# Which engine adds up weights and rows, when slots are read, and the order of row writes, in attention with a mixture of experts

## The chip, the cores and the metric

One core of one Trainium2 chip runs the whole program. The metric is the device time of one execution in microseconds (us), as the median of several runs. The engines are TensorE (PE; its weight loads are PEld), VectorE (DVE), ScalarE (ACT), GpSimd (POOL) and SyncE (SP, which here issues transfers).

## The reference

```python
def _attn_ref(q, k, v, sampled_blocks) -> np.ndarray:
    ...
    scores = scale * np.matmul(q, k.transpose(0, 1, 3, 2))
    ...
    scores = np.where(mask, scores, -1000000000.0)
    ...
    return np.matmul(attn, v).astype(np.float32)
def _moe_ref(x, w_gate, w_noise, noise, w1, w2) -> np.ndarray:
    ...
    logits = x @ w_gate
    noise_scale = np.log1p(np.exp(x @ w_noise))
    noisy_logits = logits + noise_scale * noise
    top2 = np.argpartition(-noisy_logits, 2, axis=1)[:, :2]
    ...
    for e in range(E):
        for k in range(2):
            mask = top2[:, k] == e
            ...
            h = np.maximum(x[mask] @ w1[e], 0.0)
            out[mask] += top2_w[mask, k, None] * (h @ w2[e])
```

The attention has 4 batches of 8 heads, 768 positions of 64, in blocks of 32; its mask leaves each block the blocks beside it, the first, the last and three sampled ones. The rows of its output, with all heads side by side, are the x of the experts: 3072 rows of 512. There are 8 experts (512 to 1024 to 512), and the two weights of a row are a softmax over its two largest gates.

## The kernel before

The first part, up to some 350 us, is the attention; beside it the router picks two experts for each row and scatters, for each expert, row numbers and weights into a table in DRAM (`slots`). The second part runs the experts as **units**: u0 and u1 are two shares of expert 0, u2 is expert 1, and u3 to u8 are experts 2 to 7. A unit has up to 816 rows: six chunks of 128 and one of 48. All products are done in f16 with each f32 operand split into a high and a low half, so that one product is three matmuls.

For a unit, the program reads its slots (`meta`, tile `mt`), makes row numbers of them (`indices`, tile `gi`, on VectorE), gathers the rows of x (`gather`, tile `xg`, an indirect transfer on GpSimd's queue) and transposes them by transfers on SyncE's queue (`xpose`, tiles `xta` and `xtb`). `gather_prev` fetches the rows of the output that earlier units have written (`pv`, GpSimd's queue). **Layer 1** makes h in the tiles `hh` and `hl`. **Layer 2** (`mm2`) makes each chunk of output rows in the PSUM bank `pc`; `finish` weighs it and adds `pv` on VectorE (tile `y`, three buffers), and writes the rows by an indirect transfer on GpSimd's queue (`out_dram<-y,mt`). The narrow chunk of 48 rows is done second, turned after the third, so that two writes come together there.

u0 to u2 do layer 1 straightforwardly (`mm1`, in the order `FORDER`). u3 to u8 are **fast units** (`layer1_fast`): layer 1 is done in 2 x 2 blocks with seven products in place of eight (28 products of 6 matmuls, in the order of the list `PRODUCTS`; the first digit is the group, the second the product). This takes sums and differences of weight blocks (`weight_sums`, tile `ws`, four additions of 256 columns for each of four pieces) and of x (`row_sums`, four of 816 columns; `row_differences`, eight of 408 columns; tile `xf`, one buffer, filled once for each half s of the rows' columns). `row_high` and `row_low` split `xf` into the tile `tb`, on ScalarE and VectorE. Products 4 to 7 read `tb`; the fourth product in the list is the first of these. Inside a group, ScalarE copies partial results into tiles `ta` and `tc`, two buffers each, VectorE adds to them, and `high` and `low` make `hh` and `hl` of them.

Weight pieces (eight of 512 KB an expert) are loaded into `wraw`, three buffers; the high half is made on ScalarE (`high_piece`), the low half on VectorE (`low_piece`), and then the load three pieces on is issued on SyncE (`next_load`).

Every engine works through its own instructions in the order in which the program was written; an engine that waits holds up all that stands behind on it. What is done beside the matmuls is written out in tables: `FRONT` and `FRONT_ROWS` at eight places (hooks) in layer 1, `BACK0` (u2) and `BACK` (u3 on) after each chunk of layer 2. In them h and l are the high and low half of a weight piece, s its sums, g a gather and x a transpose for a unit ahead, rs, rd, rh, rl the row sums, differences, high and low half for the next unit. u2 thus prepares u3 in `BACK0`, where both halves of its rows stand in layer 2; later units do half 0 in layer 1 and half 1 in layer 2. The slots of a unit are read two units ahead, at the third hook of layer 1, and `indices` follows at the fourth. The tiles of `meta` have three buffers, and a buffer is free when the writes of its unit have landed.

## Time and profile before

| | us |
|---|---|
| median of 3 runs | 972.69 (970.95 to 973.55) |
| the profiled run | 964.51 |
| span of the profiled run, first to last instruction | 962.7 |
| PE busy in the span | 830.0 (86%) |
| DVE, ACT, POOL busy | 541.2, 367.0, 467.4 |

Mean granted TensorE clock of the span: 0.94 of full speed. Layer 1 of u2 begins at 443.01 us, its layer 2 at 483.79, u3 at 518.30, and the last matmul ends at 946.8.

How to read the rows below. A row of the timeline has start and duration in us, engine, line, operation, what it writes and reads, a count, and in brackets how long the engine stood idle before and what ended that. SPq, POOLq and the like are an engine's own instruction queue. A row of waits has the waiting engine, tile and line, what it waited for, the total us, the number of times and the longest. A row of a stretch has its bounds, its length, the busy us (and instructions) of PE, PEld, DVE, ACT and POOL, the granted clock as a share of full speed, the DMA share and GB/s. A row of a source line has the operation with its count, and the shortest, median and longest duration in ns. L790 is line 790 of the kernel before.

### The profile page before, as it was taken

The numbers are of one execution on the slowest core, as the hardware profiler recorded it, in microseconds if no ns is written. First come the engines' busy times: TensorE is split into PE (matmuls) and PEld (weight loads), VectorE is DVE, ScalarE is ACT, GpSimd is POOL, SyncE is SP. The second block draws the span as 40 slices with busy tenths as digits, with TensorE's granted clock in tenths as the row PEclk, the third lists the DMA queues.
The fourth block names the chain that finished last, engine by engine and source line by source line (L and its number), as shares of the span: only waits on it lengthen the run. The fifth ranks groups of instructions, "written<-read, shape, count | busy, mean of one in ns | idle before, by whom it ended". The sixth has DMA issues, their size and how long they took to land. (4 is left out here: it accounts for less than half of the span.)

```text
span 962.7 us, 25081 instructions
## 1 busy us (share of the span) xinstructions
PE 830.0 (86%) x9999; PEld 508.6 (53%) x9999; DVE 541.2 (56%) x1088; ACT 367.0 (38%) x672; POOL 467.4 (49%) x758
## 2 busy tenths in 40 slices
PE   5988988888987879985998699898898898999993
PEld 3776766676665756462553354454453453554551
DVE  5666755774564547131457475676675574776620
ACT  5657545544534424020323342532532441533500
POOL 3553465357338312533447636567556556645320
PEclk9999999988878889997999899999998998999997
DMA  7776779677318879448757727837737637832311
GB/s 210 189 203 175 208 194 179 158 190 164 92 41 148 243 170 334 114 154 173 197 127 154 185 85 151 215 114 160 201 105 151 170 109 149 212 103 98 93 36 36
DMA packets 121649, 149.01 MB, mean 155 GB/s; under 512 B 72370, under 2 KB 79283, under 8 KB 121522
## 3 DMA queue, kind: packets, MB, share of 16 engines
q1 hardware_dynamic: 107810, 109.50, 47.4%
q0 software_dynamic: 13712, 37.81, 13.8%
q8 instruction: 81, 1.33, 0.6%
q14 instruction: 46, 0.38, 0.1%
HBM read 107.14 MB, written 26.32 MB: 139 GB/s over the span
## 5 line engine op out<-in xcount | busy, mean ns | idle before, releaser
L1025 PE MATMUL pc<-w,hh 128*128 128x512 f16 x768 | 232.6, 385 | 13.6 <-DVE y L1057 11.5
L1058 POOL DMA_INDIRECT out_dram<-y,mt x56 | 76.4, 1365 | 206.6 <-DVE y L1057 86.7
L978 PEld LDWEIGHTS <-w 128*128 128x128 f16 x1008 | 99.9, 99 | 106.1 <-issue 31.2
L1025 PE MATMUL pc<-w,hl 128*128 128x512 f16 x384 | 147.6, 384 | 0.5 <-DVE hl L950 0.4
L1025 PEld LDWEIGHTS <-hh 128*128 128x128 f16 x768 | 75.3, 99 | 103.5 <-issue 19.5
L273 ACT ACTIVATE p<-ps,m 128x256 f32<-128x256 f32 x192 | 75.3, 475 | 75.4 <-DVE m L270 68.0
L270 DVE TENSOR_REDUCE m<-ps 128x2 f32<-128x512 f32 x96 | 61.8, 685 | 49.6 <-PE ps L224 40.4
L818 DVE SCALAR_TENSOR_TENSOR w<-wraw,w 128x1024 f16<-128x1024 f32 (+1 forms) x62 | 70.2, 1132 | 20.3 <-ACT w L814 20.3
L224 PE MATMUL ps<-kk,q 64*32 64x192 f32 (+1 forms) x1920 | 76.7, 338 | 4.2 <-issue 4.2
L881 POOL DMA_INDIRECT xg<-x_rows,gi x56 | 70.1, 1252 | 20.4 <-issue 12.1
L319 PE MATMUL po<-vb,ptr 128*32 128x68 f32 x1536 | 64.2, 231 | 17.9 <-issue 17.5
L185 POOL COPY kk<-kk 128x128 f32 x264 | 65.0, 296 | 28.9 <-PE ps L224 22.5
L715 POOL DMA_INDIRECT slots<-r_pay,r_sl x48 | 48.0, 1001 | 57.0 <-DVE r_ot L707 48.1
L899 POOL DMA_INDIRECT pv<-out_dram,gi x49 | 52.5, 1071 | 38.5 <-issue 23.5
L319 PE MATMUL po<-va,ptr 128*32 128x68 f32 x1536 | 60.1, 233 | 9.4 <-issue 7.6
L224 PEld LDWEIGHTS ps<-kk,q 64*32 64x32 f32 (+1 forms) x1920 | 51.5, 129 | 30.0 <-issue 24.5
L978 PE MATMUL pa<-tb,w 128*128 128x408 f16 x288 | 57.5, 337 | 9.7 <-ACT tc L966 4.3
L814 ACT ACTIVATE w<-ws 128x1024 f16<-128x1024 f32 x24 | 25.2, 1051 | 106.0 <-POOL ws L790 106.0
L1057 DVE SCALAR_TENSOR_TENSOR y<-pc,mt,pv 128x512 f32<-128x512 f32 x42 | 31.3, 746 | 58.3 <-PE pc L1025 56.0
L1025 PEld LDWEIGHTS <-hl 128*128 128x128 f16 x384 | 38.0, 99 | 48.5 <-issue 3.3
L297 PE MATMUL ps<-r_ident,p 128*128 128x128 f32 x384 | 61.6, 312 | 0.0
L947 ACT ACTIVATE hh<-pa 128x408 f16<-128x408 f32 (+2 forms) x48 | 22.3, 467 | 99.7 <-PE pa L939 94.8
(196 smaller groups left out, 1556.4 us busy)
## 6 DMA issues: line engine op xcount, KB each, us to landing
wraw<-in_moe_w_dram SPq DMA_DIRECT2D x64, 512.0 KB
va<-in_vw_dram SPq DMA_DIRECT2D x16, 768.0 KB
vb<-in_vx_dram SPq DMA_DIRECT2D x176, 64.0 KB
q<-in_qt_dram SPq DMA_DIRECT2D x24, 256.0 KB
out_dram<-zero SPq DMA_DIRECT2D x8, 768.0 KB
va<-in_vx_dram SPq DMA_DIRECT2D x88, 64.0 KB
va<-in_vw_dram SPq DMA_DIRECT2D x8, 576.0 KB
kk<-in_kt_dram SPq DMA_DIRECT2D x9, 512.0 KB
```

Of the source, the lines that this page charges most:

```text
L185: nc.gpsimd.tensor_copy(kk[:, self.row(t, j) + n], flat[:, bass.ds(v[j, n] * P, P)])
L224: mm = lambda o, l, r: nc.tensor.matmul(o, l, r, start=True, stop=True, skip_group_check=True)
L270: nc.vector.tensor_reduce(m[:, par], s[par].rearrange("p (e c) -> p e c", e=2), axis=AX.X, op=ALU.max, negate=True)
L273: nc.scalar.activation(p[:, 2 * e + par], s[par][:, 256 * e:256 * e + 256], AF.Exp, bias=m[:, par, e:e + 1])
L297: nc.tensor.transpose(t[:, e, c], p[:, 2 * e + par, P * c:P * c + P], self.ident)
L319: nc.tensor.matmul(o[32 * j:32 * j + 32, h], d[:, h % 2, h // 2, x, 32 * j:32 * j + 32], self.values(v[:, self.slot(t, j)], 4 * f + h), st ...
L818: self.nc.vector.scalar_tensor_tensor(lo, t, WS, hi, op0=ALU.mult, op1=ALU.subtract)
L881: nc.gpsimd.indirect_dma_start(out=self.xg[0:m, c], out_offset=None, in_=self.x_dram[0:nr], in_offset=bass.IndirectOffsetOnAxis(ap=r["gi"] ...
L899: nc.gpsimd.indirect_dma_start(out=self.pv[0:m, c, :], out_offset=None, in_=self.out, in_offset=bass.IndirectOffsetOnAxis(ap=r["gi"][0:m, ...
L978: nc.tensor.matmul(o, w[:, wt, slot, s * P:s * P + P], mv(s, a), start=i == 0 and p in tail, stop=i == 5, skip_group_check=True)
L1025: nc.tensor.matmul(py, h[:, f, o], w(f)[:, x], start=i == 0, stop=i == last)
L1058: nc.gpsimd.indirect_dma_start(out=self.out, out_offset=bass.IndirectOffsetOnAxis(ap=r["mt"][0:m, c, 0:1], axis=0), in_=y[0:m], in_offset= ...
```

## The change

`weight_sums` moves from GpSimd to VectorE; `row_sums` and `row_differences` move from VectorE to GpSimd. The tile pool of the slots has nine buffers in place of three, and the slots of u4 to u8 are all read in u2's layer 1, with their `indices` there and after u2's first chunk. The writes of rows of one unit are declared independent of one another. The orders `FORDER` and `PRODUCTS` and the tables change; the half-1 row sums of a fast unit stand two steps earlier in layer 2. A load follows its `low_piece` one step later, at the start of the next entry (list `freed`).

```diff
-FORDER = (0, 4, 1, 5, 6, 2, 7, 3)
-PRODUCTS = [(int(a), int(b)) for a, b in ("01 11 02 06 07 17 16 05 14 21 12 04 26 03 15 25 22 31 27 13 36 37 24 35 "
-                                           "32 23 34 33").split()]
+FORDER = (0, 4, 1, 5, 6, 7, 2, 3)
+PRODUCTS = [(int(a), int(b)) for a, b in ("01 11 02 06 12 21 07 16 05 17 04 15 03 14 22 27 26 31 13 24 36 25 37 35 "
+                                           "32 34 23 33").split()]
...
-        self.mp = pool("mmeta", 3)
+        self.mp = pool("mmeta", 9)
...
-        tt = lambda x, y, z, op: nc.gpsimd.tensor_tensor(x, y, z, op=op)
+        tt = lambda x, y, z, op: nc.vector.tensor_tensor(x, y, z, op=op)
...
-        self.nc.vector.tensor_tensor(self.st["xf", u, s][:, j].rearrange("p k c -> p (k c)"), v(0), v(1), op=ALU.add)
+        self.nc.gpsimd.tensor_tensor(self.st["xf", u, s][:, j].rearrange("p k c -> p (k c)"), v(0), v(1), op=ALU.add)
...
-        tt = lambda o, a, b: self.nc.vector.tensor_tensor(o, a, b, op=ALU.subtract)
+        tt = lambda o, a, b: self.nc.gpsimd.tensor_tensor(o, a, b, op=ALU.subtract)
...
-        nc.gpsimd.indirect_dma_start(
+        d = nc.gpsimd.indirect_dma_start(
...
+        for p in r.setdefault("done", []):
+            self.tc.declare_no_dep(d.ins, p.ins, reason="a unit has every row once")
+        r["done"].append(d)
...
-    FRONT_ROWS = ((("x", -6),), (("x", -7),), (), (("rs", 0, 0),), (), (("rs", 0, 1),), (("rd", 0, 0),), (("rd", 0, 1),))
-    BACK0 = ((("h", 0), ("l", 0), ("s", 1)),
-             (("h", 1), ("g", 0)),
-             (("l", 1), ("s", 2), ("rs", 0, 0), ("rs", 0, 1), ("g", 1), ("g", 2)),
-             (("h", 2), ("rd", 0, 0), ("rd", 0, 1), ("rh", 0), ("l", 2), ("s", 3), ("g", 3), ("x", 0)),
-             (("rl", 0), ("rs", 1, 0), ("rs", 1, 1), ("g", 4), ("x", 1), ("x", 2)),
-             (("h", 3), ("rd", 1, 0), ("rd", 1, 1), ("rh", 1), ("l", 3), ("g", 5), ("x", 3)),
+    FRONT_ROWS = ((("x", -6),), (("x", -7),), (), (), (("rs", 0, 0),), (("rs", 0, 1),), (("rd", 0, 0),), (("rd", 0, 1),))
+    BACK0 = ((("h", 0), ("l", 0), ("s", 1), ("h", 1)),
+             (("l", 1), ("g", 0)),
+             (("s", 2), ("h", 2), ("rs", 0, 0), ("rs", 0, 1), ("g", 1), ("g", 2)),
+             (("rd", 0, 0), ("rd", 0, 1), ("rh", 0), ("l", 2), ("s", 3), ("h", 3), ("g", 3), ("x", 0)),
+             (("l", 3), ("rl", 0), ("rs", 1, 0), ("rs", 1, 1), ("g", 4), ("x", 1), ("x", 2)),
+             (("rd", 1, 0), ("rd", 1, 1), ("rh", 1), ("g", 5), ("x", 3)),
              (("rl", 1), ("g", 6), ("x", 4)))
-    BACK = ((("h", 0), ("rh", 0), ("l", 0), ("s", 1), ("g", 0), ("g", 1)),
-            (("h", 1), ("rl", 0), ("g", 2)),
-            (("l", 1), ("s", 2), ("g", 3), ("x", 0)),
-            (("h", 2), ("rs", 1, 0), ("rs", 1, 1), ("l", 2), ("s", 3), ("g", 4), ("x", 1), ("x", 2)),
-            (("rd", 1, 0), ("rd", 1, 1), ("rh", 1), ("g", 5), ("x", 3)),
-            (("h", 3), ("l", 3), ("rl", 1), ("g", 6), ("x", 4)),
+    BACK = ((("h", 0), ("rh", 0), ("l", 0), ("s", 1), ("h", 1), ("g", 0), ("g", 1)),
+            (("rl", 0), ("l", 1), ("rs", 1, 0), ("rs", 1, 1), ("g", 2)),
+            (("s", 2), ("h", 2), ("rd", 1, 0), ("g", 3), ("x", 0)),
+            (("l", 2), ("s", 3), ("h", 3), ("rd", 1, 1), ("g", 4), ("x", 1), ("x", 2)),
+            (("l", 3), ("rh", 1), ("g", 5), ("x", 3)),
+            (("rl", 1), ("g", 6), ("x", 4)),
             ())
...
+    freed = []
...
-        next_load(e, i)
+        freed.append((e, i))
...
-            if u + 2 < nu:
-                if f == 2:
-                    ex.meta(u + 2)
-                if f == 3:
-                    ex.indices(u + 2)
+                if f + 2 > FAST and f + 2 < nu:
+                    ex.meta(f + 2)
+                if f > FAST and f < nu:
+                    ex.indices(f)
...
+        while freed:
+            next_load(*freed.pop(0))
...
+                for v in range(ex.FB, nu):
+                    ex.indices(v)
```

How the change moves instructions, at three places. In the rows below a bracket names the counters that an instruction waits for: DVE, ACT, PE and Pool count the instructions of an engine, DMAHW the transfers of SyncE's queue, and DMASW0 to DMASW7 those of GpSimd's queue, in turn; x4 is four alike.

GpSimd in layer 2 of u2, where u3 is prepared, from the writes of the second and third chunk on. Before (`ws` are the sums of weights, `xg` the gathered rows of u4):

```order
L1058 DMA out_dram<-y,mt 3072x512 [waits DMASW5_49,DMASW3_49,DVE_49]
L1058 DMA out_dram<-y,mt 3072x512 [waits DMASW6_49,DMASW5_49,DVE_49]
L790 TENSOR_TENSOR ws<-wraw 128x256 [waits DMAHW5_49,DVE_49]
L790 TENSOR_TENSOR ws<-ws,wraw 128x256 [waits Pool_49]
L790 TENSOR_TENSOR ws<-wraw 128x256
L790 TENSOR_TENSOR ws<-wraw,ws 128x256 [waits Pool_49]
L881 DMA xg<-x_rows,gi 128x1024 [waits DMAHW0_49,DMASW7_49]
```

Now (`xf` are the row sums and differences of u3):

```order
L1058 DMA out_dram<-y,mt 3072x512 [waits DMASW5_49,DVE_49]
L1058 DMA out_dram<-y,mt 3072x512 [waits DMASW6_49,DVE_49]
L829 TENSOR_TENSOR xf<-xtb 128x816 [waits DMAHW5_49,DMAHW6_49,DMAHW3_49,DMAHW7_49,DMAHW2_49,PE_49]
L829 TENSOR_TENSOR xf<-xtb 128x816
L881 DMA xg<-x_rows,gi 128x1024 [waits DMASW7_49]
L881 DMA xg<-x_rows,gi 128x1024 [waits DMASW0_49]
L1058 DMA out_dram<-y,mt 3072x512 [waits DMASW1_49,DVE_49]
L833 TENSOR_TENSOR xf<-xf 128x408 [waits Pool_49] x4
L881 DMA xg<-x_rows,gi 128x1024 [waits DMASW2_49]
L1058 DMA out_dram<-y,mt 3072x512 [waits DMASW3_49,DVE_49]
L829 TENSOR_TENSOR xf<-xtb 128x816 [waits DVE_49,Activation_49]
L829 TENSOR_TENSOR xf<-xtb 128x816
```

The sums of weights are gone from GpSimd, the row operations stand in their place, and a write no longer waits for the counter of the write before it; the second pair of row sums waits for VectorE and ScalarE, which read the buffer's first filling.

GpSimd in layer 2 of u3, up to its last three writes. Before:

```order
L790 TENSOR_TENSOR ws<-wraw 128x256 [waits DMAHW1_49,DVE_49]
L790 TENSOR_TENSOR ws<-ws,wraw 128x256 [waits Pool_49]
L790 TENSOR_TENSOR ws<-wraw 128x256
L790 TENSOR_TENSOR ws<-wraw,ws 128x256 [waits Pool_49]
L881 DMA xg<-x_rows,gi 128x1024
L1058 DMA out_dram<-y,mt 3072x512 [waits DMASW7_49,DMASW1_49,DVE_49]
L881 DMA xg<-x_rows,gi 128x1024 [waits DMASW2_49]
L1058 DMA out_dram<-y,mt 3072x512 [waits DMASW3_49,DMASW1_49,DVE_49]
L881 DMA xg<-x_rows,gi 48x1024 [waits DMAHW3_49]
L1058 DMA out_dram<-y,mt 3072x512 [waits DMASW3_49,DVE_49]
```

Now:

```order
L833 TENSOR_TENSOR xf<-xf 128x408 [waits Pool_49] x2
L881 DMA xg<-x_rows,gi 128x1024 [waits DMASW0_49]
L1058 DMA out_dram<-y,mt 3072x512 [waits DMASW1_49,DVE_49]
L881 DMA xg<-x_rows,gi 128x1024 [waits DMASW2_49]
L1058 DMA out_dram<-y,mt 3072x512 [waits DMASW3_49,DVE_49]
L881 DMA xg<-x_rows,gi 48x1024 [waits DMASW4_49]
L1058 DMA out_dram<-y,mt 3072x512 [waits DMASW5_49,DVE_49]
```

Each write now waits for VectorE and for a counter that was last used eight transfers earlier, and no longer for the counter of the write before it.

VectorE in layer 1 of u3, before:

```order
L950 SCALAR_TENSOR_TENSOR hl<-tc,hh 128x816 [waits Activation_49]
L869 TENSOR_SCALAR gi<-mt 128x6 [waits DMAHW4_49]
L869 TENSOR_SCALAR gi<-mt 48x1 [waits DMAHW5_49]
L829 TENSOR_TENSOR xf<-xta 128x816 [waits DMAHW3_49,DMAHW7_49,DMAHW1_49,DMAHW0_49]
L967 TENSOR_TENSOR tc<-pa,tc 128x408 [waits PE_49]
L950 SCALAR_TENSOR_TENSOR hl<-pa,hh 128x408 [waits Activation_49]
```

Now:

```order
L967 TENSOR_TENSOR tc<-pa,tc 128x408 [waits PE_49,Activation_49]
L950 SCALAR_TENSOR_TENSOR hl<-tc,hh 128x816 [waits Activation_49]
L967 TENSOR_TENSOR tc<-pd,tc 128x408 [waits PE_49]
L950 SCALAR_TENSOR_TENSOR hl<-pa,hh 128x408 [waits Activation_49]
L967 TENSOR_TENSOR ta<-pc,ta 128x408 [waits PE_49]
L950 SCALAR_TENSOR_TENSOR hl<-tc,hh 128x816 [waits Activation_49]
```

The row numbers and the row sums are gone from this place.

## Rows read from the trace of the kernel before

**Rows 1.** The chain that ended last: its shares of the span by line.

```profile
by line: DMA out_dram<-y,mt 9.2%; issue 7.3%; PE pc L1025 6.9%; PE pa L978 4.1%; POOL ws L790 2.6%; PE pd L978 2.4%; POOL xg L881 2.0%; DVE w L818 1.6%; DVE hl L950 1.3%; DVE xf L833 1.2%; ACT hh L947 1.0%; ACT w L814 0.9%; DVE y L1057 0.7%
```

**Rows 2.** Stretches: the two layers of u3, then u4, u5, u6, u7.

```profile
518.30:562.19 43.89, 33.02 (x170) 17.33 (x168) 27.35 (x37) 17.17 (x26) 21.42 (x20) 0.88 0.69 162
562.19:598.15 35.96, 34.09 (x246) 16.89 (x245) 22.03 (x27) 10.78 (x13) 23.18 (x21) 1.00 0.53 119
598.15:668.07 69.92, 64.05 (x413) 33.25 (x412) 47.15 (x59) 26.82 (x40) 41.49 (x38) 1.00 0.65 159
668.07:742.87 74.80, 66.28 (x414) 34.01 (x412) 47.76 (x61) 28.68 (x42) 42.81 (x38) 0.95 0.64 154
742.87:818.06 75.19, 67.43 (x413) 34.38 (x412) 45.99 (x60) 27.28 (x39) 41.85 (x38) 0.93 0.60 148
818.06:882.25 64.19, 63.40 (x413) 33.35 (x412) 44.07 (x56) 26.14 (x39) 36.93 (x33) 1.00 0.49 140
```

**Rows 3.** Waits of TensorE from 518.3 to 946.8 us, the longest four in total.

```profile
PE pa L978 <- DVE hl L950: 13.5, 3, 6.8
PE pc L1025 <- DVE y L1057: 11.1, 4, 3.6
PE pa L978 <- ACT tc L966: 4.3, 6, 0.7
PE pa L978 <- DVE tb L848: 3.5, 3, 1.6
```

**Rows 4.** Timeline around 545 us, u3's layer 1: SyncE, VectorE, TensorE.

```profile
541.95 0.43 SPq L856 DMA_DIRECT2D mt<-slots  x1
546.22 0.62 DVE L869 TENSOR_SCALAR gi<-mt 128x6 int32<-128x6 int32 x2 [6.94 <-DMA mt<-slots]
548.92 1.52 PE L978 MATMUL pa<-xtb,w 128*128 128x408 f16 x4 [6.76 <-DVE hl L950]
```

**Rows 5.** Timeline around 805 us, u6's layer 2: GpSimd, ScalarE, VectorE, TensorE.

```profile
803.34 0.92 POOL L1058 DMA_INDIRECT out_dram<-y,mt  x1 [5.73 <-DMA out_dram<-y,mt]
807.23 1.06 ACT L814 ACTIVATE w<-ws 128x1024 f16<-128x1024 f32 x1 [14.89 <-POOL ws L790]
808.32 1.23 DVE L818 SCALAR_TENSOR_TENSOR w<-ws,w 128x1024 f16<-128x1024 f32 x1 [8.56 <-ACT w L814]
810.26 1.01 PE L1025 MATMUL pc<-w,hh 128*128 128x512 f16 x2 [3.63 <-DVE y L1057]
```

**Rows 6.** A stretch of 6.8 us around the stop at 548.92.

```profile
546.00:552.80 6.80, 3.88 (x12) 1.72 (x12) 5.42 (x9) 1.83 (x3) 6.28 (x6) 0.50 0.60 219
```

**Rows 7.** Source lines: additions of weights on GpSimd, differences of rows on VectorE.

```profile
L790 POOL TENSOR_TENSOR ws<-wraw x48: 718/752/2262, 476.4 to 877.4; 128x256 f32<-128x256 f32 x48
L790 POOL TENSOR_TENSOR ws<-wraw,ws x24: 723/727/1709, 478.7 to 878.4; 128x256 f32<-128x256 f32 x24
L833 DVE TENSOR_TENSOR xf<-xf x48: 570/585/1123, 503.0 to 878.9; 128x408 f32<-128x408 f32 x48
```

**Rows 8.** Source lines from 480 to 962 us: writes and gathers on GpSimd.

```profile
L1058 POOL DMA_INDIRECT out_dram<-y,mt x49: 907/1146/5114, 490.2 to 947.9; - x49
L881 POOL DMA_INDIRECT xg<-x_rows,gi x35: 944/1043/2975, 495.1 to 824.4; - x35
```

**Rows 9.** Timeline of u2's layer 2 and u3's start; a tb in u6.

```profile
490.20 1.51 POOL L1058 DMA_INDIRECT out_dram<-y,mt  x1 [10.77 <-DVE y L1057]
497.79 5.11 POOL L1058 DMA_INDIRECT out_dram<-y,mt  x1 [1.71 <-DVE y L1057]
523.39 0.86 PE L978 MATMUL pa<-tb,w 128*128 128x408 f16 x4 [1.82 <-ACT ta L966]
525.83 0.50 PE L978 MATMUL pa<-tb,w 128*128 128x408 f16 x1 [1.57 <-DVE tb L848]
523.92 1.85 DVE L848 TENSOR_TENSOR tb<-xf,tb 128x1632 f16<-128x1632 f32 x1
782.87 1.56 ACT L844 ACTIVATE tb<-xf 128x1632 f16<-128x1632 f32 x1
```

## The prediction

> **What bounds the kernel now.** I read the chain that ended last first [rows 1]: its largest share, 9.2%, is the landing of writes of output rows, a transfer that nothing computes. Then I read the second half unit by unit [rows 2]. The units on experts 2 to 7 (I call them u3 to u8) do the same matmuls, yet the stretches from u3's start to u7's end last 79.9 (43.89 + 35.96), 69.9, 74.8, 75.2 and 64.2 us, and TensorE is busy 63.4 of u7's 64.2. So TensorE's own work bounds a unit at about 64, and u3 to u6 carry 43 us of something else. The waits of TensorE in these units [rows 3] say what: 13.5 us for VectorE's low halves of h, 11.1 for its output rows y, 4.3 for a copy on ScalarE, 3.5 for the low halves of the row sums (tb).
>
> Two of these have one cause each. **The slots.** In every fast unit VectorE stands at gi until the slots of a unit two ahead are read; SyncE issued that read only at 541.95, VectorE had waited 6.94 us when it went on at 546.22, and TensorE stood 6.76 us behind it [rows 4]. **The writes.** A write of rows waits for the landing of the write before: GpSimd stood 5.73 us so; behind the write in its queue are the sums of weights, for which ScalarE had waited 14.89 us, VectorE 8.56, and TensorE at last 3.63, since the bank pc waited for y [rows 5]. The granted clock is 0.50 in the stretch around the stop at 548.92 [rows 6]; TensorE had idled before it fell.
>
> **The change part by part.** The run with the profile took 964.5 us (span 962.7); the median of the runs is 972.7. I sum in us against the profiled run and take the same us off the median. Nothing ahead of 483 us moves by more than places in SyncE's queue (four more reads of slots, each some 0.4 us of issue [rows 4], and loads one step later); I cost that at nothing, because three weight pieces are in flight, and at 6 us if one load came late, once.
>
> *Slots early.* All gi are done in u2; the wait at gi goes, and with it the 13.5 us and part of the low clock. What is next late there is listed below.
>
> *Writes in free order.* The writes of a unit lose the wait for one another, as the order shows; they keep the one on y and on a counter that comes round after eight transfers. GpSimd's 5.7 us waits go.
>
> *Sums of weights on VectorE.* 16 additions of 256 columns a unit leave GpSimd. There one takes 0.727 in the median [rows 7]. On VectorE 408 columns take 0.585 [rows 7], so a sum takes at most that: 16 x 0.585 = 9.4. VectorE loses 8 differences (8 x 0.585 = 4.7) and 4 sums of 816 columns that cost at least as much each (2.3). So VectorE gains at most 2.4 us a unit; it was busy 44 to 48 of 64 to 75 [rows 2], and I cost that at nothing. What counts is that ScalarE and VectorE no longer wait for GpSimd here.
>
> *Row sums on GpSimd.* 4 sums of 816 columns and 8 differences of 408 a unit. No row shows these on GpSimd. In proportion to 0.727 for 256 columns a difference takes 1.16 and a sum 2.3, and a fixed part can only lower that; as fast as on VectorE the difference would take 0.585. I take 1.1 and 2.1, near the upper end, since it is the same operation on the same engine: 17 us a unit, for 16 x 0.73 = 12 that leave. The upper end with contention is the longest addition, 2.26 [rows 7], three times the median.
>
> Now what is late next. Layer 1 reads tb in its fourth product; VectorE makes tb's second half (1.85), after ScalarE (1.56), after GpSimd's last differences, which stand behind writes (1.15 + 0.3 between two) and gathers (1.04 + 0.3) [rows 8, 9].
>
> In a **fast unit** the chain is, from the start of layer 2 (0): first write at 6.4 (as 490.20 is to 483.79 [rows 2, 9]); write, two gathers, two sums, a gather: 1.45 + 2.7 + 4.2 + 1.3, to 16.1; two writes 2.9, two differences 2.2, gather 1.3, write 1.45, two differences 2.2, to 26.2; then 1.56 and 1.85: 29.6. The sums also wait for VectorE to be done with the first half, some 2 us more: 32. Layer 2 ends at 34.3 to 34.5 and the fourth product comes 3 us later, at 37.4. About 5 us to spare: no wait.
>
> In **u2**, which prepares u3, it does not fit. There all twelve row operations stand in layer 2's last four chunks. Counted from the two writes at 497.8 [rows 9]: writes 2.9, sums 4.2, gathers 2.7, write 1.45, four differences 4.4: 513.4. ScalarE's first half 1.56, and behind it in its queue the split of the fourth weight piece, 2.0 (two parts, the second 1.06 [rows 5]); VectorE's low part of that 1.23 and tb's first half 1.85: 520.1. Only now may GpSimd refill the single buffer: sums 4.2, gather 1.3, write 1.45, differences 4.4: 531.5; then 1.56 and 1.85: 534.9. TensorE needs it at 521.6, where it stands already today (523.39 less 1.82 [rows 9]), for 1.82 + 1.57 = 3.4. The new wait is 13.3, and the clock falls behind such a wait: after 548.92 some 4 us at half speed [rows 6], 2 to 3 us lost; I take 2.5. So u3 loses the wait at gi and gets this instead.
>
> *The order of products.* The 0.7 us for ScalarE's copy (six times, 4.3 [rows 3]) is the third group's buffer "tc" waiting for the first group's; in the new order the first group ends one product earlier and the third starts its buffer three later. I count 0.7 a unit as gone, and nothing else.
>
> **Sum.** A free unit: u7's 64.2 - 0.7 = 63.5. u3: 63.5 + 13.3 + 2.5 = 79.3 for 79.9, -0.6. u4 -6.4, u5 -11.3, u6 -11.7, u7 and u8 -0.7 each. Together -31.4. I leave 1 us in each of u4 to u6 for a tb that is late now and then (today it is, by about 1 us): +3. So -28.4: 936 for the profiled run, 972.7 - 28.4 = **944 us** for the median.
>
> Two rules of the Trainium skill speak against the change, in sentences that the sum does without. The page "GPSIMD Engine Reference", section 3.1, has a two-input addition 1.96 times slower there than on VectorE; the trace agrees (0.727 for 256 columns against 0.585 for 408 is twice per column). By its 4497 ns for 2048 columns, an estimate, a difference takes 0.9 and a sum 1.8; the four sums and eight differences of u2's chain would then be 2.8 us shorter and the time 941.
>
> **Rivals.** *A short chain.* Were a difference and a sum on GpSimd nearly as quick as on VectorE, or did the writes and gathers run ahead, u3 would wait about as today (3.4, and no further clock loss): 13.3 + 2.5 - 3.4 = 12 less, 932. Against it: the median of 0.727.
>
> *The engines block one another.* VectorE now has additions from SBUF just where GpSimd has its row operations. The trace shows the price of meeting: the additions on GpSimd go from 0.727 to 2.26 at worst, VectorE's differences from 0.585 to 1.12 [rows 7]. If each row operation takes half as long again (1.6 and 3.1), u2's chain grows by 4 x 1.0 + 8 x 0.5 = 8 and the fast unit's by 2.0 + 2.0 = 4, with slower gathers beside it 6 to 8, which uses up its 5 us: 1 to 3 us of wait in each of u4 to u6 beyond those allowed. 944 + 8 + 3 x 2.5 = 960. The Trainium skill, page "SBUF — State Buffer", section "Who interferes with whom", has the rule: a VectorE instruction with two inputs in SBUF and a GpSimd instruction that reads SBUF contend, and the one that comes first holds the port to its end. The longest additions in the trace agree with it.
>
> *Slower: GpSimd becomes the bound.* A unit has 21 transfers on it, 7 writes at 1.15 and 14 gathers at 1.04 [rows 8] and 0.3 between, 29, some 4 us of waiting for landings before old rows are read, and the row operations. u3 to u7 last 364 us today, 72.8 a unit; GpSimd passes that when its row operations take 72.8 - 33 = 40 us a unit, 2.3 times my 17. At the worst multiple seen, 3.1, it would be 33 + 53 = 86 a unit: 5 x 13 = 65 slower, 1038. The decisive place is the shared stretch of layer 2. Of the additions in the trace few show such a price, as their medians say [rows 7].
>
> *It does not do what it says.* The writes may be free to start and still land one behind the other, some 5.7 us each: then y, with three buffers, holds layer 2 to 7 x 5.7 = 40 in place of 34.3, and u4 to u6 keep 3 x 5.7 of what they should lose: 961. The gathers, issued 1.3 apart without a wait, speak against it.
>
> **How the numbers follow.** Forecast (one long wait at u3, then free units) 0.52; short chain 0.18; engines blocking 0.18; writes landing singly 0.04; GpSimd the bound 0.06; a mixture that ends about where it began 0.02. The range 931 to 960 takes in the first three, 0.88, and loses some of it to their tails: 0.8. About 0.3% (2.9 us) can be told from no change: faster 0.92, same 0.02, slower 0.06.
>
> **What would show it.** No wait of VectorE at gi after 500 us. No write that waits for a write of its unit. One wait of TensorE of 10 to 16 us for tb at u3's start, behind GpSimd's differences; units u4 to u6 of 63 to 66 us at a clock near 1.00; no wait for the copy to "tc". Row operations on GpSimd of 1.0 to 1.3 and 1.9 to 2.4. I am wrong if u3's wait is under 5 or over 20, or if tb holds the later units as well.

## The result, and the profile after the change

| | before | after |
|---|---|---|
| median of 4 runs, us | 972.68 (970.95 to 973.55) | 938.56 (937.82 to 948.15) |
| ratio after / before | | 0.9674, 95% interval 0.961 to 0.9738 |
| the profiled run (span), us | 964.51 (962.7) | 938.22 (936.4) |
| from u2's layer 2 to the last matmul, us | 463.0 | 430.2 |

The changed kernel is faster by 34.1 us at the median, and the forecast of 944 lies 5.4 us above it. The profiled run of before was 8 us below its median and that of after at its median, so the two traces differ by only 26.3 us. They differ in three places: 32.8 us less in the part that the change touches (from u2's layer 2 at 483.79 and 488.21 us to the last matmul), 4.4 us more ahead of it, and 2.0 more behind the last matmul (15.9 and 17.9 us). In the eleven kernels below the beginning of u2's layer 2 lies anywhere from 485.9 to 501.9 us, and no run here shows why. So I compare kernels by two numbers: the measured time, and the part from u2's layer 2 to the last matmul in the trace, which I call the **tail**. A tail is from one execution, and no kernel was traced twice, so a difference of a few us between two tails counts only where the waits in the traces show it. Medians in us take in every run; ratios leave out the runs in the slower of two states that executions of one kernel show.

Part 4 of the page of after, the chain that ended last, by engine (beside [rows 1]). The landing of output writes, 9.2% of the span before, is among the 2% of DMA now:

```profile
PE 75%; DVE 9%; issue 7%; ACT 3%; POOL 2%; DMA 2%; SPq 1%; POOLq 0%; DVEq 0%; ACTq 0%
```

The stretches of after that answer to [rows 2]: the two layers of u3, then u4, u5, u6, u7, and last the stretch around u3's long wait:

```profile
522.15:565.28 43.13, 32.24 (x169) 17.18 (x168) 23.93 (x29) 17.19 (x28) 30.89 (x24) 0.84 0.54 142
565.28:599.21 33.93, 33.93 (x245) 16.89 (x244) 31.23 (x35) 11.25 (x14) 25.02 (x16) 1.00 0.62 165
599.21:662.13 62.92, 62.92 (x414) 33.35 (x413) 51.52 (x61) 27.04 (x39) 46.08 (x34) 1.00 0.61 173
662.13:727.11 64.98, 63.06 (x413) 33.35 (x412) 54.87 (x61) 27.05 (x39) 45.47 (x34) 1.00 0.62 170
727.11:792.05 64.94, 63.07 (x413) 33.31 (x412) 54.82 (x61) 26.93 (x39) 45.21 (x34) 1.00 0.65 169
792.05:854.97 62.92, 62.92 (x414) 33.34 (x413) 48.19 (x61) 26.93 (x39) 41.18 (x30) 1.00 0.51 145
528.70:542.30 13.60, 5.83 (x17) 2.50 (x18) 3.75 (x5) 4.79 (x7) 10.80 (x11) 0.50 0.60 121
```

In u4 and u7 TensorE is busy for the whole unit: 62.92 of 62.92. u5 and u6 are 2 us longer, and u3 keeps 10.9 us beyond the 32.24 in which TensorE is busy. The waits of TensorE in after that come to more than 0.2 us, from 522 to 918 us (beside [rows 3]):

```profile
PE pa L978 <- ACT ta L966: 10.7, 1, 10.7
PE pd L978 <- ACT tc L966: 3.8, 2, 1.9
```

The timeline of after around u3's start, GpSimd, ScalarE, VectorE and TensorE, in the order of the chain (beside [rows 9]):

```profile
502.22 1.61 POOL L1058 DMA_INDIRECT out_dram<-y,mt  x1 [3.27 <-DVE y L1057]
505.06 3.43 POOL L829 TENSOR_TENSOR xf<-xtb 128x816 f32<-128x816 f16 x2
513.17 4.42 POOL L833 TENSOR_TENSOR xf<-xf 128x408 f32<-128x408 f32 x4
517.62 1.56 ACT L844 ACTIVATE tb<-xf 128x1632 f16<-128x1632 f32 x1 [12.48 <-POOL xf L833]
522.04 1.85 DVE L848 TENSOR_TENSOR tb<-xf,tb 128x1632 f16<-128x1632 f32 x1
524.04 3.41 POOL L829 TENSOR_TENSOR xf<-xtb 128x816 f32<-128x816 f16 x2 [3.93 <-DVE tb L848]
530.00 4.42 POOL L833 TENSOR_TENSOR xf<-xf 128x408 f32<-128x408 f32 x4
534.45 1.56 ACT L844 ACTIVATE tb<-xf 128x1632 f16<-128x1632 f32 x1 [13.59 <-POOL xf L833]
535.92 0.89 ACT L966 ACTIVATE ta<-pa 128x408 f32<-128x408 f32 x2
536.47 0.86 PE L978 MATMUL pa<-tb,w 128*128 128x408 f16 x2 [10.67 <-ACT ta L966]
```

This is the prediction's chain for u2, step by step: half 0's sums and differences on GpSimd, ScalarE's high half, VectorE's low half at 522.04, and only then GpSimd's sums for half 1 at 524.04, after 3.93 us of standing still. ScalarE's copy to "ta" stands behind the second high half in its queue, and TensorE waits for that copy. The granted clock is 0.50 from 528.70 to 542.30: TensorE idled first, and after it went on at 536.47 it ran 5.8 us at half speed, which loses 2.9.

The source lines of after from 480 to 940 us (shortest, median and longest ns, beside [rows 7] and [rows 8]):

```profile
L833 POOL TENSOR_TENSOR xf<-xf x48: 1042/1082/1917, 513.2 to 846.0; 128x408 f32<-128x408 f32 x48
L829 POOL TENSOR_TENSOR xf<-xtb x12: 1721/1734/1756, 505.1 to 772.2; 128x816 f32<-128x816 f16 x12
L829 POOL TENSOR_TENSOR xf<-xta x12: 1722/1736/2715, 550.1 to 834.9; 128x816 f32<-128x816 f16 x12
L790 DVE TENSOR_TENSOR ws<-wraw x48: 404/419/1264, 489.9 to 846.1; 128x256 f32<-128x256 f32 x48
L950 DVE SCALAR_TENSOR_TENSOR hl<-ta,hh x24: 582/584/5523, 539.0 to 883.2; 128x408 f16<-128x408 f32 x24
L818 DVE SCALAR_TENSOR_TENSOR w<-ws,w x24: 1210/2064/4624, 495.3 to 849.2; 128x1024 f16<-128x1024 f32 x24
```

In the median a difference takes 1.08 us on GpSimd, a sum 1.73, a sum of weights on VectorE 0.42; at worst a difference takes 1.92 and a sum 2.72. The last two rows are low halves, made on VectorE. A low half of h ("hl") that takes 0.58 in the median took 5.52 at worst. Of the low halves of the weight sums (L818), the 14 of 24 that ran beside additions on GpSimd took 2.06 or more, 4.62 at worst, and the other ten at most 1.23; before, all were near 1.22:

```profile
L818 DVE SCALAR_TENSOR_TENSOR w<-ws,w x24: 1209/1219/1255, 490.7 to 883.2; 128x1024 f16<-128x1024 f32 x24
```

The timeline of after at the low half of 5.52 us, in u5, VectorE, GpSimd, ScalarE, TensorE:

```profile
679.73 5.52 DVE L950 SCALAR_TENSOR_TENSOR hl<-ta,hh 128x408 f16<-128x408 f32 x1 [0.37 <-issue]
680.39 3.42 POOL L829 TENSOR_TENSOR xf<-xta 128x816 f32<-128x816 f16 x2
683.76 5.52 POOL L833 TENSOR_TENSOR xf<-xf 128x408 f32<-128x408 f32 x4
688.75 0.88 ACT L947 ACTIVATE hh<-tc 128x816 f16<-128x816 f32 x1 [3.23 <-DVE tc L967]
690.08 0.68 PE L978 MATMUL pd<-tb,w 128*128 128x408 f16 x3 [1.92 <-ACT tc L966]
```

The low half ends only when GpSimd's two sums and its first difference are done. Behind it VectorE's addition to "tc" is late, ScalarE waits 3.23 for that, its next copy to "tc" stands behind, and TensorE waits 1.92. The same happens in u6, where the low half takes 5.48 and TensorE waits until 755 us. These are the 2 us of u5 and u6.

### The profile page after: what moved, and what is told of

The parts are those of the page before. It is cut to its first block, busy times and chain, and to the rows that moved or that the text cites. A ratio compares the mean times of both kernels' runs of the same rounds, so it can differ in the third digit from the quotient of the medians.

```text
span 936.4 us, 25004 instructions
## 1 busy us (share of the span) xinstructions
PE 820.1 (88%) x9999; PEld 507.8 (54%) x9999; DVE 568.3 (61%) x1112; ACT 366.7 (39%) x672; POOL 485.5 (52%) x734
## 3 DMA queue, kind: packets, MB, share of 16 engines
q0 software_dynamic: 13712, 37.81, 13.5%
## 4 chain that ended last, share of the span: by engine, by line
PE 75%; DVE 9%; issue 7%; ACT 3%; POOL 2%; DMA 2%; SPq 1%; POOLq 0%; DVEq 0%; ACTq 0%
PE pc L1025 24%; PE pa L978 10%; PE ps L224 9%; PE po L319 7%; PE ps L297 5%; PE pd L978 5%; PE pa L939 3%; PE pd L939 3%; PE pc L1034 2%; PE pc L978 2%; PE pog L345 2%; DVE m L270 2%; DVE w L818 2%; PE ps L285 1%; PE po L389 1%
## 5 line engine op out<-in xcount | busy, mean ns | idle before, releaser
L1025 PE MATMUL pc<-w,hh 128*128 128x512 f16 x768 | 228.4, 379 | 1.9 <-issue 1.9
L1058 POOL DMA_INDIRECT out_dram<-y,mt x56 | 70.0, 1250 | 149.9 <-DVE y L1057 73.8
L1025 PE MATMUL pc<-w,hl 128*128 128x512 f16 x384 | 145.5, 379 | 0.3 <-issue 0.3
L273 ACT ACTIVATE p<-ps,m 128x256 f32<-128x256 f32 x192 | 75.2, 474 | 73.7 <-DVE m L270 65.9
L818 DVE SCALAR_TENSOR_TENSOR w<-wraw,w 128x1024 f16<-128x1024 f32 (+1 forms) x62 | 84.5, 1362 | 14.4 <-ACT w L814 13.9
L881 POOL DMA_INDIRECT xg<-x_rows,gi x56 | 76.3, 1362 | 22.0 <-issue 13.0
L319 PE MATMUL po<-vb,ptr 128*32 128x68 f32 x1536 | 64.8, 236 | 14.0 <-issue 13.6
L978 PE MATMUL pa<-tb,w 128*128 128x408 f16 x288 | 56.7, 340 | 10.7 <-ACT ta L966 10.7
L833 POOL TENSOR_TENSOR xf<-xf 128x408 f32<-128x408 f32 x48 | 62.5, 1301 | 2.6
```

The lines of the kernel that those rows point to most:

```text
L273: nc.scalar.activation(p[:, 2 * e + par], s[par][:, 256 * e:256 * e + 256], AF.Exp, bias=m[:, par, e:e + 1])
L319: nc.tensor.matmul(o[32 * j:32 * j + 32, h], d[:, h % 2, h // 2, x, 32 * j:32 * j + 32], self.values(v[:, self.slot(t, j)], 4 * f + h), st ...
L818: self.nc.vector.scalar_tensor_tensor(lo, t, WS, hi, op0=ALU.mult, op1=ALU.subtract)
L833: tt = lambda o, a, b: self.nc.gpsimd.tensor_tensor(o, a, b, op=ALU.subtract)
L881: nc.gpsimd.indirect_dma_start(out=self.xg[0:m, c], out_offset=None, in_=self.x_dram[0:nr], in_offset=bass.IndirectOffsetOnAxis(ap=r["gi"] ...
L978: nc.tensor.matmul(o, w[:, wt, slot, s * P:s * P + P], mv(s, a), start=i == 0 and p in tail, stop=i == 5, skip_group_check=True)
```

## The experiments

The parts of the change were put into the kernel before one by one (e1 to e3, e11) or taken back out of the changed kernel (e4 to e7); e8 to e10 move the row operations to VectorE again. Each group ran on one chip with its own runs of the kernel before, and the ratios are against those: their medians were 976.86 us beside e1 to e4, 973.02 beside e5 to e8, and 970.97 beside e9 to e11. So a time of one group is not to be divided by the 972.68 of the table.

| kernel | us | ratio (95%) | tail |
|---|---|---|---|
| before | 972.68 | | 463.0 |
| e1 early slots alone | 972.68 | 0.9919 (0.9856 to 0.9981) | 460.6 |
| e2 free writes alone | 945.09 | 0.9696 (0.9592 to 0.98) | 427.7 |
| e3 both | 944.50 | 0.9678 (0.954 to 0.9816) | 432.7 |
| e11 free writes, new orders | 938.80 | 0.9722 (0.9657 to 0.9787) | 424.4 |
| after | 938.56 | 0.9674 (0.961 to 0.9738) | 430.2 |
| e4 after, engines as before | 950.73 | 0.9792 (0.9714 to 0.9871) | 431.4 |
| e5 after, writes as before | 952.59 | 0.9809 (0.9719 to 0.99) | 439.1 |
| e6 after, slots as before | 943.04 | 0.9657 (0.9532 to 0.9782) | 428.4 |
| e7 after, orders as before | 949.91 | 0.9804 (0.9728 to 0.9879) | 440.6 |
| e8 after, u3's rows on VectorE | 937.96 | 0.9668 (0.9592 to 0.9744) | 424.7 |
| e9 as e8, and half 0 of all units | 923.73 | 0.9539 (0.9488 to 0.9591) | 412.9 |
| e10 after, all rows on VectorE | 927.37 | 0.9537 (0.9466 to 0.9608) | 414.2 |

The first three kernels tell the two waits apart that the prediction put at the head of its sum.

**e1: the slots alone,** in the kernel before.

```diff
-        self.mp = pool("mmeta", 3)
+        self.mp = pool("mmeta", 9)
...
-            if u + 2 < nu:
-                if f == 2:
-                    ex.meta(u + 2)
-                if f == 3:
-                    ex.indices(u + 2)
+                if f + 2 > FAST and f + 2 < nu:
+                    ex.meta(f + 2)
+                if f > FAST and f < nu:
+                    ex.indices(f)
...
+                for v in range(ex.FB, nu):
+                    ex.indices(v)
```

> The kernel before with one part of the change: nine buffers for the slots, all slots read in u2. My theory: VectorE's wait at gi (16.2 us after 500 us) and TensorE's 13.5 us behind it go, the waits for y (11.1 us) stay: 15 us and some low clock less than 972.7, so 953 to 960. Rival (the chain of writes decides, and the wait moves to it): the waits for y and tb grow by what gi loses, and the time is 967 to 973.

The tail fell by 2.4 us only. The waits of e1 from 518 to 946 us, VectorE, GpSimd, TensorE:

```profile
DVE xf L829 <- DMA xta<-xg: 11.6, 3, 7.4
POOL out_dram L1058 <- DMA out_dram<-y,mt: 41.4, 12, 6.2
PE pa L978 <- DVE tc L967: 6.6, 1, 6.6
```

VectorE no longer waits at gi, and stands instead at the row sums of the next unit, for transposed rows, 7.4 us at worst; TensorE still has one wait of 6.6 at that place. The writes of e1 hold GpSimd as they did. The time is the rival's, but what the wait moved to was not y or tb, as the rival had it (11.8 and 1.6 us).

**e2: the free writes alone,** in the kernel before.

```diff
-        nc.gpsimd.indirect_dma_start(
+        d = nc.gpsimd.indirect_dma_start(
...
+        for p in r.setdefault("done", []):
+            self.tc.declare_no_dep(d.ins, p.ins, reason="a unit has every row once")
+        r["done"].append(d)
```

> The kernel before with one part of the change: the writes of a unit in free order. My theory: the waits of GpSimd for a write (36.1 us) and TensorE's 11.1 us for y go, and the slots, whose buffers come free earlier, are read a little sooner: 955 to 962. Rival (writes land one behind the other anyway): y waits for its buffers instead, 968 to 975.

The tail fell by 35.3 us, more than in the whole change. The tail of e2 as one stretch, and waits of TensorE (from 500 us) and VectorE (from 535 us) in it:

```profile
501.90:929.60 427.70, 416.94 (x2719) 217.22 (x2716) 288.69 (x366) 162.94 (x237) 253.34 (x217) 1.00 0.60 148
PE pa L978 <- DVE tc L967: 2.6, 2, 2.0
DVE gi L869 <- DMA mt<-slots: 4.2, 3, 2.5
```

The time is 10 us under the theory's range. All waits of TensorE in the tail come to 10.7 us in place of 36.9, and its busy time falls from 425.94 to 416.94 as the granted clock goes from 0.97 to 1.00: together the 35. The largest of the waits left, 2.6 us, are what remains of the 13.5 behind gi, though the read of the slots was not moved: it stands where it did in SyncE's queue, and comes 11 to 17 us after the start of u3 to u6 where before it came 17 to 24. Why is in the trace of before, a few us ahead of [rows 4], on GpSimd and SyncE:

```profile
533.96 1.02 POOL L1058 DMA_INDIRECT out_dram<-y,mt  x1 [3.61 <-DVE tc L967]
535.28 0.94 POOL L881 DMA_INDIRECT xg<-x_rows,gi  x1 [0.31 <-issue]
540.50 1.26 SPq L891 DMA_TRANSPOSE xta<-xg  x1
```

The last write of u2 holds GpSimd until 533.96, the last gather stands behind it, SyncE's transpose of the gathered rows waits for the gather, and the read of the slots at 541.95 [rows 4] stands behind that transpose. So the wait at gi is the end of the same chain of queues that begins with a write. Reading the slots earlier takes the last link away, and VectorE then stops at the transposed rows, which come out of the same chain. (That the bracket of the write names an instruction of VectorE is the rule that the last event gets the wait; in e2 it is the write's counter that is missing.)

**e3: both.** The edits of e1 and e2 together.

> The kernel before with both: slots early and writes in free order, engines and tables as before. My theory: both waits are the whole gain and the move of additions between engines gives nothing, since GpSimd's sums of weights were late only behind the writes: 932 to 942, u3's wait for tb 3 to 4 us. Rival (the move of additions is needed to take the sums out of GpSimd's queue): 945 to 955, with ScalarE still waiting for ws and TensorE for y.

944.5 us, as e2, and a tail of 432.7. The time lies between the ranges of theory and rival, and the early slots add nothing to the free writes. TensorE has two waits of 4.9 us in sum for VectorE's low halves, in u5 and u7. Ahead of them VectorE stands at the row sums, for the transposed rows, as in e1 (3.97 and 2.59 us; from 518 to 925 us):

```profile
DVE xf L829 <- DMA xta<-xg: 6.9, 3, 4.0
```

So the early slots trade the rest of the wait at gi for a wait one step earlier in the chain.

**e4: the additions on the engines of before,** in the changed kernel, with its new tables.

```diff
-        tt = lambda x, y, z, op: nc.vector.tensor_tensor(x, y, z, op=op)
+        tt = lambda x, y, z, op: nc.gpsimd.tensor_tensor(x, y, z, op=op)
...
-        self.nc.gpsimd.tensor_tensor(self.st["xf", u, s]
+        self.nc.vector.tensor_tensor(self.st["xf", u, s]
...
-        tt = lambda o, a, b: self.nc.gpsimd.tensor_tensor(o, a, b, op=ALU.subtract)
+        tt = lambda o, a, b: self.nc.vector.tensor_tensor(o, a, b, op=ALU.subtract)
```

> The changed kernel with the additions back on the engines they were on before (sums of weights on GpSimd, sums and differences of rows on VectorE), everything else as changed. My theory: u3's wait of 10.7 us with its low clock and the two waits of 1.9 us in u5 and u6 go: 924 to 930. Rival (sums of weights on GpSimd hold up ScalarE and VectorE again): 940 to 950.

u3's layer 1 falls to 36.9 us, as it should without GpSimd in its chain, but the layers 2 of u3 to u7 are now 35.8 in place of 33.9. The waits of TensorE in e4, and two rows of ScalarE's timeline:

```profile
PE pr L1044 <- ACT yt L1038: 9.8, 6, 1.7
586.95 1.06 ACT L814 ACTIVATE w<-ws 128x1024 f16<-128x1024 f32 x1 [6.19 <-POOL ws L790]
587.91 0.31 ACT L1038 ACTIVATE yt<-pc 128x192 f32<-128x192 f32 x1
```

In the new tables the high half of piece 1 stands ahead of the copy "yt" of the narrow chunk in ScalarE's queue. Made on GpSimd, the sums come 6.19 us too late for it; the copy waits behind and TensorE with it, six times. The tail, 431.4, is hardly longer than that of after (430.2): what u3 gains, layer 2 loses. The rest of the 12 us by which e4 is slower lies ahead of u2's layer 2 (501.2 against 488.2 us), and I have no cause for it. What the sums of weights are worth on VectorE shows against e10 below, which differs from e4 in that alone: a tail of 414.2 and a ratio of 0.9537, against 431.4 and 0.9792.

**e5: the writes in order again,** in the changed kernel.

```diff
-        for p in r.setdefault("done", []):
-            self.tc.declare_no_dep(d.ins, p.ins, reason="a unit has every row once")
-        r["done"].append(d)
```

> The changed kernel with the writes of a unit waiting for one another again. My theory: the row sums and differences on GpSimd now stand behind waits of some 5.7 us each, tb comes late in every fast unit: 5 to 10 us for each of u3 to u7, so 960 to 985. Rival (with the sums of weights off GpSimd the waits there hold up nobody): 938 to 945.

952.59 us, a ratio of 0.9809 where after has 0.9674, and a tail longer by 8.9. In the tail that is a quarter of what the same edit is worth in the kernel before (35.3), by the ratios less than half (0.0135 and 0.0304). The time is under the theory's range and above the rival's: TensorE stands behind a late tb in u3 alone, as in after, and GpSimd waits 13.7 us for writes where before it waited 36.1. In e5 the sums of weights no longer stand behind the writes in GpSimd's queue, since they are on VectorE. I take it that moving the sums was a second way to break the same chain. That is not shown by itself, since e5 also has the early slots, the new orders and the new tables. What is shown is that the gain of the free writes and that of the rest of the change don't add: in the tail the writes alone give 35.3 us, the rest alone 23.9, and both together 32.8.

**e6: the slots late again,** in the changed kernel (the edit of e1 reversed).

> The changed kernel with the slots read two units ahead through three buffers, as before. My theory: VectorE waits at gi again in u3 to u6, but the read stands less late, since writes and gathers run ahead: 2 to 4 us each, 943 to 955. Rival (freed writes alone take the wait at gi away): 937 to 941.

A ratio of 0.9657 and a tail of 428.4, with no wait of TensorE but that at u3 (10.7) and 2.1 in three others. The time is just inside the theory's range, but VectorE waits at gi only once, for 0.9 us, so it is the rival's mechanism that the trace shows. The early slots are worth nothing that can be told.

**e7: the old orders of products,** `FORDER` and `PRODUCTS` of before in the changed kernel.

> The changed kernel with the orders of products and of layer 2 as before. My theory: the wait of 0.7 us for the copy to tc comes back in each of six units: 4 us, 941 to 945. Rival (the order gives nothing, or other waits come with the new order, as the two of 1.9 us in u5 and u6): 936 to 940.

The waits of TensorE in e7:

```profile
PE pa L978 <- ACT ta L966: 15.7, 3, 10.7
PE pa L978 <- ACT tc L966: 4.4, 4, 2.2
```

The tail is 10.4 us longer. The 0.7 us for "tc" are back in three units, with 2.2 in u3, and the two waits for "ta" beside that of u3 (5.0 in sum) are in u5 and u6, where after has its 3.8. So in the changed kernel the new orders are worth more than the 4.3 that I counted; in the kernel before they give 3.3 (e11 against e2). Ahead of the waits for "ta" in u5 and u6 VectorE's low half of "tc" took 4.88 and 3.60 us beside GpSimd's additions. I take it that the new orders leave TensorE more products to do while a copy is late, which no run tries by itself.

**e8: u3's rows on VectorE.** The first of three kernels that ask what the row operations on GpSimd cost.

```diff
-        self.nc.gpsimd.tensor_tensor(self.st["xf", u, s]
+        (self.nc.vector if u == FAST else self.nc.gpsimd).tensor_tensor(self.st["xf", u, s]
...
-        tt = lambda o, a, b: self.nc.gpsimd.tensor_tensor(o, a, b, op=ALU.subtract)
+        tt = lambda o, a, b: (self.nc.vector if u == FAST else self.nc.gpsimd).tensor_tensor(o, a, b, op=ALU.subtract)
```

> The changed kernel with the row sums and differences of u3 alone on VectorE, those of u4 to u8 on GpSimd as changed. My theory: TensorE's wait of 10.7 us at u3's start with some 3 us at low clock falls to 0 to 3 us: 925 to 930. Rival (the wait comes from the order of steps in u2's layer 2, not from the engine): 935 to 940, with ScalarE still late for tb.

u3's layer 1 takes 30.7 us in place of 43.1, and its wait falls to 0.3. But the time is 937.96, no better than after, and the tail fell by 5.5 where u3 alone gave 12.4 back. TensorE's waits in e8, and the place in u5, VectorE and GpSimd:

```profile
PE pd L978 <- ACT tc L966: 8.0, 4, 2.3
673.06 5.97 DVE L950 SCALAR_TENSOR_TENSOR hl<-tc,hh 128x816 f16<-128x816 f32 x1
673.75 3.42 POOL L829 TENSOR_TENSOR xf<-xta 128x816 f32<-128x816 f16 x2
677.12 6.16 POOL L833 TENSOR_TENSOR xf<-xf 128x408 f32<-128x408 f32 x4
```

The wait for "tc" now comes in u3, u5, u6 and u7, 8.0 in all. The layers 1 of u5 to u7 take 98.1 us in place of 91.1, which is the 7 us that are missing. The units run the same instructions, but the low half that meets GpSimd's additions is now the wider one, 1.01 us alone and 5.97 here. That the shift in time brought it to that place is read from the two timelines, not tried by itself.

**e9: half 0 on VectorE in all units, half 1 on GpSimd.** Half 0 is what runs in layer 1, beside the low halves of h.

```diff
-        self.nc.gpsimd.tensor_tensor(self.st["xf", u, s]
+        (self.nc.vector if u == FAST or s == 0 else self.nc.gpsimd).tensor_tensor(self.st["xf", u, s]
...
-        tt = lambda o, a, b: self.nc.gpsimd.tensor_tensor(o, a, b, op=ALU.subtract)
+        tt = lambda o, a, b: (self.nc.vector if u == FAST or s == 0 else self.nc.gpsimd).tensor_tensor(o, a, b, op=ALU.subtract)
```

> The changed kernel with the row sums and differences of u3 and of half 0 (the half that later units do in layer 1) on VectorE, those of half 1 on GpSimd. From u2's layer 2 to the last matmul the changed kernel took 430.2 us, with u3's rows alone on VectorE 424.7, with waits of 1.0 to 2.3 us for the copy to tc in u4 to u7. My theory: those waits come from VectorE's low half of ta, held up to 5.5 us while GpSimd adds rows; without additions on GpSimd in layer 1 they go: 415 to 418 there. Rival (VectorE is simply full in layer 1): the waits stay or grow with 9 us more work on it, 424 to 432.

The tail of e9, the only waits of TensorE over 0.1 us in it, and the source lines of the low halves of h and of the weight sums:

```profile
488.10:901.00 412.90, 412.30 (x2719) 217.34 (x2716) 314.15 (x428) 163.25 (x237) 206.99 (x155) 1.00 0.57 154
PE pa L978 <- DVE tb L848: 0.4, 1, 0.4
PE pc L1034 <- issue: 0.2, 1, 0.2
L950 DVE SCALAR_TENSOR_TENSOR hl<-ta,hh x24: 582/583/654, 527.5 to 865.8; 128x408 f16<-128x408 f32 x24
L818 DVE SCALAR_TENSOR_TENSOR w<-ws,w x24: 1210/1643/4612, 495.2 to 832.0; 128x1024 f16<-128x1024 f32 x24
```

TensorE is busy for 412.30 of 412.90 us at a granted clock of 1.00; the longest low half of "ta" is 0.65 us. GpSimd's additions for half 1 still hold VectorE in layer 2, where a low half of weight sums takes up to 4.61 us, but TensorE does not wait for it. 923.73 us is the shortest time of the study, and its interval lies below that of after. What is left of this part is TensorE's own work.

**e10: all row operations on VectorE,** so that only the sums of weights have changed engines (from GpSimd to VectorE).

> The changed kernel with all row sums and differences and all sums of weights on VectorE; GpSimd adds nothing. My theory: VectorE has some 55 of a unit's 63 us and meets no additions on GpSimd: 414 to 420 from u2's layer 2 to the last matmul (430.2 in the changed kernel), u3's wait 0 to 2. Rival (VectorE becomes the bound in layer 2): waits for y or tb of 2 to 4 us a unit, 425 to 435.

927.37 us and the same ratio as e9. The tail of e10:

```profile
494.70:908.90 414.20, 412.61 (x2718) 217.29 (x2716) 303.86 (x458) 163.48 (x237) 163.04 (x125) 1.00 0.57 153
```

VectorE does 30 instructions more than in e9 and is busy for 10 us less. In after it does 42 fewer than in e9 and is busy for 309.93: work taken from VectorE to GpSimd came back as longer instructions on VectorE. An estimate of how much: without its 72 row operations (48 of 0.58 and 24 of 1.00 us, 52) VectorE's 303.86 of e10 would be 252, so that some 58 of the 309.93 of after are time in which its instructions were held. With e4 and after, e10 also prices the two moves of additions in the tail: the sums of weights on VectorE give 17.2 (431.4 to 414.2), the row operations on GpSimd take 16.0 of it back (414.2 to 430.2), 13.6 of them in u3.

**e11: the free writes and the new orders of products,** in the kernel before.

> The kernel before with two lines of the change: the writes of a unit in free order, and the new orders of products and of layer 2. From u2's layer 2 to the last matmul the free writes alone took 427.7 us, with six waits of 0.7 for the copy to tc. My theory: the new order takes these away: 421 to 424. Rival (the new order suits only the new tables): waits for tc or for weights in other places, 427 to 432.

A tail of 424.4, 3.3 less than e2, and at 0.9722 no faster than e2 by the interval. It has 4.4 us of waits of TensorE at products to "pd", in u3 and u6, that the profile puts down to issue. Ahead of them VectorE stands at gi, 2.97 and 3.71 us, and ScalarE's copy to "tc" comes late behind it. In u6, VectorE:

```profile
742.93 0.32 DVE L869 TENSOR_SCALAR gi<-mt 128x6 int32<-128x6 int32 x2 [3.71 <-DMA mt<-slots]
```

So with slots read late a part of that wait is left. Even so, two parts of the change, a few lines, give all of its time that can be told.

## Why the prediction was right, and where not

The units in us, each from the start of its layer 1 to the end of its layer 2, as the prediction summed them:

| | before | after | change | predicted |
|---|---|---|---|---|
| u2's layer 2 | 34.5 | 33.9 | -0.6 | 0 |
| u3 | 79.9 | 77.1 | -2.8 | -0.6 |
| u4 | 69.9 | 62.9 | -7.0 | -6.4 |
| u5 | 74.8 | 65.0 | -9.8 | -11.3 |
| u6 | 75.2 | 64.9 | -10.3 | -11.7 |
| u7 | 64.2 | 62.9 | -1.3 | -0.7 |
| u8 | 64.6 | 63.5 | -1.1 | -0.7 |
| allowance | | | | +3 |
| sum (before rounding) | | | -32.8 | -28.4 |

- **What bounds a unit** was right: TensorE's own work. A free unit was taken at 63.5 and is 62.9; its layer 2 is 33.9 where the clean ones of before were 34.3.
- **u3's new wait** was right in kind, place and chain, and 2.6 us too long: 13.3 foretold, 10.7 measured. A difference was taken at 1.1 and measured 1.08; a sum was taken at 2.1 and measured 1.73, which makes the chain's four sums 1.5 shorter. And TensorE went on with ScalarE's copy, 0.5 after ScalarE's high half, before VectorE's low half (1.85) was done. The clock's 2.5 were 2.9. From the 4497 ns for 2048 columns in the Trainium skill, "GPSIMD Engine Reference", section 3.1, a difference was estimated at 0.9 and a sum at 1.8: the trace agrees for the sum and is 0.2 above it for the difference.
- **The two causes** were one. I had the slots and the writes as separate waits with a part of the gain each. e1 and e2 show that the wait at gi was the end of the queue behind the writes. That the sum didn't suffer is luck: both parts are in the change. But "with gi goes 13.5" would have been wrong by 11 us for a change that only reads the slots early. The step that failed is the one that took the last waiting instruction, the read at 541.95, for the cause, without asking what held SyncE before it.
- **The sums of weights on VectorE** cost no wait of TensorE, as costed: 0.42 each. But VectorE's busy time, taken to grow by at most 2.4 us a unit, grew by 4.1 to 8.8 in u4 to u7 (in u5 from 47.76 to 54.87), since its instructions were held by GpSimd's. And I did not see what the move is worth with the new tables, 17.2 in the tail (e10 against e4).
- **The orders** were costed at 4.3; e7 has 10.4 for them in the changed kernel, e11 has 3.3 in the kernel before. Slack against a late ScalarE, which I had counted at nothing, would explain the difference; it is argued, not shown.
- **The allowance** of 3 us in u4 to u6 was near in size (3.8 measured, in u5 and u6), with the wrong mechanism, which again is luck. I expected a late tb. It was an instruction of VectorE stopped by GpSimd's row operations: the rival that the engines block one another, at a smaller price than its 16 us. I had priced that at GpSimd's row operations, which stayed at 1.08 and 1.73 in the median (1.92 and 2.72 at worst); it came on VectorE. e9 settles it: with half 0 on VectorE the low half of "ta" takes at most 0.65 us and the waits are gone.
- **GpSimd as the bound** did not happen: it is busy 45 to 46 of 63 to 65 us in u4 to u6.
- **Of the signs** named, two failed: two waits for the copy to "tc" came, 1.9 us each, and a sum took 1.73, not 1.9 to 2.4.
- **What stays open:** why u2's layer 2 begins up to 16 us earlier or later from one kernel to another, and with it the 13 us by which that start is later in e4 than in after; why e5 loses 8.9 and not 35.3; what in the new orders is worth 10.4 in e7. The free writes alone (0.9696) and the whole change (0.9674) can't be told apart.

## What to carry to other kernels

A wait that the profile names can be the end of a chain of queues: follow the engine that issued the late transfer back over what it issued before, until an instruction waits for something that is not a queue, and price an edit only against that root. When two edits break the same chain at two links, their gains don't add. Moving work from VectorE to GpSimd does not free VectorE while both add from SBUF at the same time: put on GpSimd what runs beside VectorE's reads of PSUM or its idle time, or where a held VectorE keeps TensorE waiting for nothing, as half 1 in layer 2 of e9.

## What the hardware did that was not expected

An instruction of VectorE with two inputs in SBUF (the low half from "ta" and "hh", 0.58 us) lasted 5.52 us beside additions on GpSimd, and a wider one (1.01) 5.97. It was held not for one instruction of GpSimd but for three in a row, two sums of 1.73 and the first difference of 1.04. The low half that reads PSUM ("pa") never took longer than 0.583 us in the same trace, though six of the 27 ran beside row operations of GpSimd:

```profile
L950 DVE SCALAR_TENSOR_TENSOR hl<-pa,hh x27: 567/573/583, 480.5 to 885.5; 128x408 f16<-128x408 f32 x27
```

The Trainium skill, "SBUF — State Buffer", section "Who interferes with whom", says that an instruction of VectorE with two inputs in SBUF contends with one of GpSimd that reads SBUF, and one with at most one such input, outside the modes in which VectorE uses two ports, does not. The trace agrees with both halves, 5.52 us against 0.583. That the hold goes on over several instructions of GpSimd in a row is what these rows add. Which of the two engines came first can't be told from them: VectorE's row begins 0.66 us before GpSimd's sums, longer than the 0.58 that it takes alone, and still it was VectorE that was held. In the trace of before it is the other way round: the five longest additions on GpSimd (2.26 us) each begin some 0.2 us after a low half of row sums on VectorE ("tb", 1.85 us), and that one is not stretched.
